# A two-layer attention and feed-forward kernel on one core: new planner order, spread weight loads, half-width exponentials in segment 0, and 30 matmuls on a constant tile at the start

## The chip, the cores and the metric

The kernel runs on one core of one Trainium2 chip. The metric is the device time of one execution in microseconds (us). The engines are named as the profile names them: PE (TensorE, matrix products; PEld is its weight load), ACT (ScalarE), DVE (VectorE), POOL (GpSimd) and SP (SyncE, which here issues loads, stores and transposing DMAs).

## The reference, cut to what matters

The input is 2048 tokens of width 512. Two layers are computed, with the same weights; each is an attention block followed by a gated feed-forward block, both with a layer norm in front and a residual behind:

```python
for layer in range(2):
    x = x + A(layernorm(x))      # 32 heads of width 16, 4 segments of 512 tokens
    x = x + B(layernorm(x))      # (silu(x w1) * (x w3)) w2, inner width 1376

def A(x):                         # per head
    q, k, v = x @ wq, x @ wk, x @ wv
    M, z = 0, 0                   # memory carried from segment to segment
    for s in range(4):
        p = softmax(q_s @ k_s.T / 4 + causal_mask)
        a_dot = p @ v_s
        a_mem = (phi(q_s) @ M) / (phi(q_s) @ z + 1e-6)    # phi(t) = t+1 if t>0 else exp(t)
        o_s = sigmoid(beta) * a_mem + (1 - sigmoid(beta)) * a_dot
        M, z = M + phi(k_s).T @ v_s, z + sum(phi(k_s))
    return concat(o_s) @ wo
```

## The kernel before, in words

Everything but the loads and the stores stays in SBUF. The work is cut into eight segments, numbered g = 0 to 7: four segments of 512 tokens in layer 0 and four in layer 1. A segment goes through these stages.

- **Layer norm** (`layer_norm`): DVE takes statistics of four tiles of 128 tokens (L502, L504, L507), POOL the inverse root (L509), DVE normalises (L515), and SP issues four transposing DMAs (L519) into `xa` (attention) or `xf` (feed-forward).
- **Projections** (`project`): 12 groups of four matmuls of 512 columns: four for `v` (L538), four for `q` and four for `k` (L543). ACT or DVE evicts each group (`ev`, L440 or L441). DVE makes two masked copies `km` of each `k` group (L558).
- **Memory** (`phi`, `memory_update`, `memory_read`): L564 to L645.
- **Attention** (`attention`): four head groups G, each of five *units*. One unit is a set of logits matmuls on PE (L674), one exponential of 128x2048 on ACT (L682), and one or two causal masks on POOL (L685). Two times in each G a *value group* of 16 matmuls on PE (L700) multiplies masked exponentials by `v`; the result `xs` is evicted, transposed by a DMA into `xg` (L710), divided by the row sum (L715, L718, L724), joined with the memory part (L733), and transposed by a DMA into `ot` (L735). Thus a segment has 20 units and 8 value groups.
- **Output projection** (`out_proj`, L743): 16 matmuls, then the residual on DVE (L746).
- **Feed-forward** (`ffn`): 88 matmuls for gate and up (L767), tanh on ACT (L775), two products on DVE (L777, L783), 44 matmuls down (L791), and the residual (L796). In layer 1 the result is stored by SP.

So a segment has 48 + 16 + 132 = 196 matmuls of 512 columns beside the attention units.

PSUM has two parts. Pool `S` is one slot of four banks, which holds the logits of one unit, so the next unit's logits can't be written before the exponential of the last one has been read. Pool `B` is four banks for everything else.

The order of each engine's instructions isn't written by hand. `Sched.schedule` is a list planner that runs when the kernel is built: each operation has a cost (`o_act`, `o_dve`, `o_pool`, `MM512`), a priority and possibly a *gate* (an operation that must have been placed before it), and the planner fixes one order for each engine. On the chip every engine goes through its order strictly, with semaphore waits where data is needed. An engine thus stops at a waiting instruction even if a later one could run. The planner interleaves the segments: PE fills the time of an exponential with matmuls of the projections of the next segment and of the feed-forward of earlier ones.

Loads before: the first four token tiles on SP's queue, `wq`, `wk`, `wv` and `betab` on ACT's queue at the same time (L431). `late_loads` issues everything else on POOL's queue as soon as the first transposed tiles are there: the other 12 token tiles, `wo`, `w1`, `w3`, `w2`, 6.3 MB in all. POOL then multiplies `w2` by 0.5 in place (L485, L487).

Of the kernel before, what the change touches and what calls it, by code (L numbers as in the profile page):

```python
# [13 lines left out]
H = 32  # L14
# [45 lines left out]
class Sched:  # L60
# [15 lines left out]
    def add(self, opts, fn, reads=(), writes=(), bufs=(), prio=0.0, mode=None, dmaq=None, name="", gates=(), size=0,  # L76
# [7 lines left out]
        op.issued = False  # L84
        op.eng = None
# [28 lines left out]
    def schedule(self):  # L114
# [23 lines left out]
        while left:  # L138
            best = None
            for e in ENGS:  # L140
# [3 lines left out]
                for op in avail[e]:  # L144
                    s = tf
# [180 lines left out]
def o_act(n, psum=True):  # L326
    return ("act", 114.0 + 0.833 * n, (190.0 if psum else 225.0) + 0.833 * n)


def o_dve(n, psum=False, mode=1.0):  # L330
    c = n / 0.96 / mode
    return ("dve", c + (75.0 if psum else 45.0), c + (150.0 if psum else 65.0))
# [13 lines left out]
def build(nc, A_x, A_wq, A_wk, A_wv, A_wo, A_beta, B_w1, B_w3, B_w2, out):  # L346
# [3 lines left out]
    def mkpool(name, n):  # L350
        pools[name] = Pool(name, n)
# [53 lines left out]
    mkpool("S", 1)  # L405
# [50 lines left out]
    for i in range(2):  # L456
        z = pool(lambda e, i=i: e.memset(va_r[i][:], 0.0), 3104, writes=[("va0", i)], prio=-50.0)
        o = pool(lambda e, i=i: e.memset(vheads(va_r[i], slice(0, LT), 0, H)[:, :, :, 16:17], 1.0), 128, writes=[("va0", i)], prio=-50.0)
        pools["va"].prev[i] = [z, o]

# [7 lines left out]
    ldw("act", wq_sb, A_wq, "wq", CP)  # L468
    ldw("act", wk_sb, A_wk, "wk", CP + 1)
    ldw("act", wv_sb, A_wv, "wv", CP + 2)  # L470
    dma("act", betab[:], A_beta.partition_broadcast(P), 8192, prio=CP + 3, writes=["betab"], name="ldbeta")

    def late_loads(after):
        for i in range(1, 4):
            dma("pool", x_tok[:, 4 * i:4 * i + 4, :], xv[:, 4 * i:4 * i + 4, :], 524288, prio=CP + i,
                reads=after, writes=[("x", 4 * i + j) for j in range(4)], name="ldx")
            if i == 1:
                ldw("pool", wo_sb, A_wo, "wo", CP + 1.5, reads=after)
        ldw("pool", w1_sb, B_w1, "w1", CP + 4, reads=after)
        ldw("pool", w3_sb, B_w3, "w3", CP + 5, reads=after)  # L480
        dma("pool", w2_sb[:, 0:10, :], B_w2[0:1280, :].rearrange("(t p) d -> p t d", p=P), 1310720, prio=CP + 6,
            reads=after, writes=["w2a"], name="ldw2")
        dma("pool", w2_sb[0:96, 10, :], B_w2[1280:1376, :], 98304, prio=CP + 7, reads=after, writes=["w2b"], name="ldw2")
        for a in range(2):
            pool(lambda e, a=a: e.tensor_scalar(w2_sb[:, 5 * a:5 * a + 5, :], w2_sb[:, 5 * a:5 * a + 5, :], 0.5, None, op0=ALU.mult),  # L485
                 2560, reads=["w2a"], writes=["w2a"], prio=0.9)
        pool(lambda e: e.tensor_scalar(w2_sb[0:96, 10, :], w2_sb[0:96, 10, :], 0.5, None, op0=ALU.mult), 512,  # L487
             reads=["w2b"], writes=["w2b"], prio=0.9)
# [7 lines left out]
    def layer_norm(s, name, prio, gates=(), fine=False):  # L496
# [3 lines left out]
        for i in range(LT):  # L500
            tt = 4 * s + i
            dve(lambda e, i=i, tt=tt: e.bn_stats(ln_r[st.slot][:, i, 0:6], x_tok[:, tt, :]), 512, reads=[("x", tt)],  # L502
# [9 lines left out]
        for i in range(LT):  # L512
            tt = 4 * s + i
            xn = new("xn")
            dve(lambda e, i=i, tt=tt, xn=xn: e.tensor_scalar(  # L515
                xn_r[xn.slot][:], x_tok[:, tt, :], ln_r[st.slot][:, i, 6:7], ln_r[st.slot][:, i, 9:10],
                op0=ALU.subtract, op1=ALU.mult), 512, mode=1.3, reads=[("x", tt), (st, 3, i), (st, 1, i)], writes=[(xn, 0)],
                bufs=[st, xn], prio=prio, name="norm")
# [8 lines left out]
    def project(s, g, X, first):  # L527
# [4 lines left out]
        for n, (kind, G) in enumerate(jobs):  # L532
            p0 = g - 0.95 + 0.05 * n
            B = new("B")
            for cg in range(NCG):
# [10 lines left out]
                pe(fn, MM512, reads=rd + ["w" + kind], writes=[(B, 0)], bufs=[B, X], prio=p0 + 0.001 * cg,  # L546
# [5 lines left out]
            else:  # L552
# [3 lines left out]
                if kind == "k":  # L556
                    for ee in range(2):
                        dve(lambda e, G=G, ee=ee: e.tensor_scalar(km_r[z.km.slot][:, ee, G, :], k_r[z.k.slot][:, G, :],  # L558
                                                                  cm[ee][:, 0:1], None, op0=ALU.mult), 512, mode=2.4,
# [3 lines left out]
    def phi(src, t, dst, dt_, prio):  # L563
        for hf in range(2):  # L564
# [6 lines left out]
                1024, mode=2.5, reads=rd, writes=[(dst, hf)], bufs=[src, dst], prio=prio, name="ph1")  # L571
# [3 lines left out]
                1024, mode=1.8, reads=[(x, 0), (dst, hf)], writes=[(dst, hf)], bufs=[x, dst], prio=prio, name="phmax")  # L575
# [286 lines left out]
```

The softmax here doesn't subtract the row's maximum and nothing guards it: scores larger than these inputs give would overflow.

## Time and profile before

| | |
|---|---|
| median of 3 runs | 563.25 us (562.81 to 563.76) |
| profiled execution | 562.49 us; span of the core's instructions 560.7 us |
| mean granted TensorE clock | 0.945 |
| busy share of the span | PE 86%, PEld 35%, DVE 79%, ACT 71%, POOL 42% |
| first exponential of each segment starts (us) | 20.5, 95.0, 153.3, 210.2, 263.2, 319.4, 373.2, 427.9 |
| last exponential starts | 479.9 us |

The first line is what comparisons are made against; the profiled execution is one execution of its own. A busy PE isn't a PE at its peak, since matmuls overlap and the granted clock can be half of the full one. The eight starts show how long each segment's attention lasts: 74.5 us for segment 0, 58.3 us for segment 1, and 52 to 57 us for the others. After the last exponential some 81 us remain, in which PE works off feed-forward blocks.

### The profile page before, as it was taken

The numbers are of one execution on the slowest core, as the hardware profiler recorded it, in microseconds if no ns is written. First come the engines' busy times: TensorE is split into PE (matmuls) and PEld (weight loads), VectorE is DVE, ScalarE is ACT, GpSimd is POOL, SyncE is SP. The second block draws the span as 40 slices with busy tenths as digits, with TensorE's granted clock in tenths as the row PEclk, the third lists the DMA queues.
The fourth block names the chain that finished last, engine by engine and source line by source line (L and its number), as shares of the span: only waits on it lengthen the run. The fifth ranks groups of instructions, "written<-read, shape, count | busy, mean of one in ns | idle before, by whom it ended". The sixth has DMA issues, their size and how long they took to land.

```text
span 560.7 us, 9831 instructions
## 1 busy us (share of the span) xinstructions
PE 484.8 (86%) x3836; PEld 198.4 (35%) x3904; DVE 445.5 (79%) x893; ACT 395.5 (71%) x324; POOL 235.2 (42%) x326
## 2 busy tenths in 40 slices
PE   1837568758999899999989999999999999989897
PEld 0212123222333333333333433443334433434343
DVE  4558999885769787898877989899987897868573
ACT  1736387877987799889878898888998798322130
POOL 7528843453435435545434544444454444210000
PEclk9956789877999899999999999999999999999999
DMA  5793112324211431143223231323113110220301
GB/s 169 243 275 75 39 39 47 49 49 94 39 29 30 67 67 29 29 85 58 47 39 67 49 67 39 67 48 67 39 39 85 48 40 19 67 66 1 76 0 39
DMA packets 106255, 35.31 MB, mean 63 GB/s; under 512 B 100736, under 2 KB 104832, under 8 KB 106208
## 3 DMA queue, kind: packets, MB, share of 16 engines
q1 hardware_dynamic: 102976, 26.76, 24.1%
q0 software_dynamic: 1504, 6.32, 3.2%
q10 hardware_dynamic: 1728, 1.58, 0.9%
q8 instruction: 31, 0.51, 0.4%
q14 instruction: 16, 0.13, 0.1%
HBM read 8.43 MB, written 2.10 MB: 19 GB/s over the span
## 4 chain that ended last, share of the span: by engine, by line
PE 48%; DVE 24%; DMA 11%; issue 7%; ACT 4%; POOL 4%; SPq 1%; POOLq 0%
PE psall L767 19%; PE psall L543 6%; PE psall L791 6%; DMA xg<-xs 5%; PE psall L674 5%; PE psall L700 5%; DVE xn L515 4%; ACT e L682 3%; PE psall L743 3%; PE psall L538 3%; DVE ln L502 2%; DMA ot<-og 2%; DMA pkt<-pk 1%; DVE x_tok L746 1%; DMA xf<-xn 1%
## 5 line engine op out<-in xcount | busy, mean ns | idle before, releaser
L682 ACT ACTIVATE e<-psall 128x2048 bf16<-128x2048 f32 x160 | 300.3, 1877 | 57.5 <-PE psall L674 55.1
L685 POOL TENSOR_SCALAR_AFFINE_SELECT e<-e 128x512 bf16<-128x512 bf16 x256 | 168.3, 675 | 205.7 <-ACT e L682 205.6
L767 PE MATMUL psall<-xf,w 128*128 128x512 bf16 (+1 forms) x678 | 172.5, 386 | 9.8 <-DMA xf<-xn 3.3
L767 PEld LDWEIGHTS psall<-xf,w 128*128 128x128 bf16 (+1 forms) x704 | 65.4, 101 | 90.1 <-issue 18.4
L775 ACT ACTIVATE th<-psall 128x512 bf16<-128x512 f32 (+1 forms) x88 | 52.0, 597 | 54.6 <-PE psall L767 54.5
L791 PE MATMUL psall<-w,h 128*128 128x512 bf16 (+1 forms) x334 | 87.2, 380 | 1.3 <-issue 0.8
L674 PE MATMUL psall<-q,km 32*128 32x512 bf16 (+3 forms) x1024 | 66.1, 313 | 16.0 <-ACT e L682 14.6
L777 DVE SCALAR_TENSOR_TENSOR gp<-th,psall 128x512 bf16<-128x512 bf16 (+1 forms) x88 | 59.1, 678 | 18.0 <-ACT th L775 17.4
L783 DVE TENSOR_TENSOR h<-gp,psall 128x512 bf16<-128x512 bf16 (+1 forms) x88 | 59.4, 678 | 9.2 <-PE psall L767 8.6
L700 PE MATMUL psall<-e,va 128*32 128x512 bf16 (+3 forms) x1024 | 49.2, 316 | 6.2 <-POOL e L685 5.4
L515 DVE TENSOR_SCALAR xn<-x_tok,ln 128x512 bf16<-128x512 bf16 x64 | 43.6, 713 | 12.2 <-POOL ln L509 7.6
L538 PE MATMUL psall<-wv,xa 128*128 128x512 bf16 x123 | 37.4, 418 | 14.6 <-DMA xa<-xn 13.7
L791 PEld LDWEIGHTS psall<-w,h 128*128 128x128 bf16 (+1 forms) x352 | 32.1, 98 | 38.1 <-issue 6.6
L674 PEld LDWEIGHTS psall<-q,km 32*128 32x128 bf16 x1024 | 18.0, 93 | 77.0 <-ACT e L682 66.0
L543 PE MATMUL psall<-xa,wk 128*128 128x512 bf16 x120 | 37.6, 404 | 6.8 <-DVE q L441 5.6
L502 DVE BATCH_NORM_STATS2 ln<-x_tok 128x6 f32<-128x512 bf16 x64 | 42.5, 675 | 0.4
L509 POOL TENSOR_TENSOR ln<-ln,mhalf 128x4 f32<-128x4 f32 (+1 forms) x19 | 18.2, 959 | 46.7 <-DVE ln L507 39.3
L700 PEld LDWEIGHTS psall<-e,va 128*32 128x32 bf16 x1024 | 22.3, 98 | 41.3 <-POOL e L685 21.6
L743 PE MATMUL psall<-wo,ot 128*128 128x512 bf16 x122 | 33.2, 398 | 3.6 <-DMA ot<-og 1.7
L543 PE MATMUL psall<-xa,wq 128*128 128x512 bf16 x123 | 34.2, 382 | 1.8 <-DVE va L441 1.1
L724 POOL TENSOR_TENSOR og<-xg,rd 128x256 bf16<-128x256 bf16 x27 | 20.4, 757 | 28.7 <-DVE rd L718 14.1
L796 DVE TENSOR_TENSOR x_tok<-psall,x_tok 128x512 bf16<-128x512 f32 x32 | 21.9, 684 | 13.2 <-PE psall L791 13.1
(61 smaller groups left out, 437.7 us busy)
## 6 DMA issues: line engine op xcount, KB each, us to landing
w<-in_B_w_dram POOLq DMA_DIRECT2D x2, 1376.0 KB, 11.0
out_dram<-x_tok SPq DMA_DIRECT2D x16, 128.0 KB, 1.8
x_tok<-in_A_x_dram POOLq DMA_DIRECT2D x3, 512.0 KB, 6.1
w<-in_B_w_dram POOLq DMA_DIRECT2D x1, 1280.0 KB, 16.3
xg<-xs SPq DMA_TRANSPOSE x64, 2.4
wq<-in_A_wq_dram ACTq DMA_DIRECT2D x1, 512.0 KB, 4.5
x_tok<-in_A_x_dram SPq DMA_DIRECT2D x4, 128.0 KB, 5.2
wk<-in_A_wk_dram ACTq DMA_DIRECT2D x1, 512.0 KB, 6.8
```

The costliest lines, as they stand in the source:

```text
L502: dve(lambda e, i=i, tt=tt: e.bn_stats(ln_r[st.slot][:, i, 0:6], x_tok[:, tt, :]), 512, reads=[("x", tt)], writes=[(st, 0, i)], bufs=[st], ...
L515: dve(lambda e, i=i, tt=tt, xn=xn: e.tensor_scalar(xn_r[xn.slot][:], x_tok[:, tt, :], ln_r[st.slot][:, i, 6:7], ln_r[st.slot][:, i, 9:10], ...
L538: fn = lambda e, cg=cg, G=G, B=B, st=st, sp_=sp_: e.matmul(bank(B), xa_r[X.slot][:, cg, 128 * G:128 * G + 128], wv_sb[:, cg, :], start=st, ...
L543: fn = lambda e, cg=cg, G=G, B=B, st=st, sp_=sp_, w=w: e.matmul(bank(B), w[:, cg, 128 * G:128 * G + 128], xa_r[X.slot][:, cg, :], start=st ...
L674: o = e.matmul(S4[:, pg, c:c + n], km_r[z.km.slot][32 * pg:32 * pg + 32, ee, G, 128 * j:128 * j + 128], q_r[z.q.slot][32 * pg:32 * pg + 32 ...
L682: act(lambda e, N=N, ebuf=ebuf: e.activation(e_r[ebuf.slot][:, :, 0:N], S4[:, :, 0:N], ACT.Exp, scale=SCALE), 4 * N, reads=[(sbuf_, 0)], w ...
L685: pool(lambda e, ebuf=ebuf, c=c: e.affine_select(e_r[ebuf.slot][:, :, c:c + 128], e_r[ebuf.slot][:, :, c:c + 128], pattern=[[0, 4], [1, 128]],
L700: o = e.matmul(bank(X)[32 * pg:32 * pg + 32, 128 * j:512], va_r[z.va.slot][:, j, VS * (8 * G + 2 * pg + ee):VS * (8 * G + 2 * pg + ee) + 3 ...
L767: prev = pe(lambda e, cg=cg, ft=ft, fw=fw, B=B, w=w: e.matmul(bank(B)[0:fw, :], w[:, cg, 128 * ft:128 * ft + fw], xf_r[X.slot][:, cg, :], ...
L777: dve(lambda e, fw=fw, B=B, th=th, gp=gp: e.scalar_tensor_tensor(gp_r[gp.slot][0:fw, :], th_r[th.slot][0:fw, :], 1.0, bank(B)[0:fw, :], AL ...
L783: dve(lambda e, fw=fw, B=B, gp=gp, h=hs[ft]: e.tensor_tensor(h_r[h.slot][0:fw, :], gp_r[gp.slot][0:fw, :], bank(B)[0:fw, :], ALU.mult), 51 ...
L791: prev = pe(lambda e, i=i, ft=ft, fw=fw, B=B, h=hs[ft]: e.matmul(bank(B), h_r[h.slot][0:fw, 128 * i:128 * i + 128], w2_sb[0:fw, ft, :], st ...
```

## The change

The main parts, in the order of the program:

- POOL clears only one of the two `va` buffers at the start, and DVE the other. DVE also sets one `h` buffer to 0.25, and 30 matmuls of 512 columns on that constant tile are PE's first instructions. Nothing reads their result.
- `wv`, `wq`, `wk` are issued on ACT's queue only when the four token tiles have landed, `betab` first. The load of `wo` moves to the head of POOL's queue.
- The other loads on POOL's queue are cut into smaller pieces and gated on units of segment 0, so that POOL issues them among its masks.
- The factor 0.5 moves from `w2` into the product that makes `h` (a `scalar_tensor_tensor` in place of a `tensor_tensor`); POOL's three multiplications fall away.
- Pool `S` gets two slots of two banks. In segment 0 each unit is cut in two halves: half of the logits matmuls, an exponential of 128x1024, then the other half. In all other segments a unit takes both slots, as before.
- Half of the joins with the memory part (L733) go to POOL by the planner's choice.
- The planner's costs, priorities and gates change, and so does the order on every engine, through all eight segments.

The core of the diff (the costs and priorities shown stand for some more of their kind):

```diff
-    mkpool("S", 1)
+    mkpool("S", 2)
...
-        z = pool(lambda e, i=i: e.memset(va_r[i][:], 0.0), 3104, writes=[("va0", i)], prio=-50.0)
+        z = (dve if i == 0 else pool)(lambda e, i=i: e.memset(va_r[i][:], 0.0), 3104, writes=[("va0", i)], prio=-50.0 if i == 0 else 0.5)
...
+    wset = dve(lambda e: e.memset(h_r[0][:], 0.25), 512, writes=["warm"], prio=CP - 1)
+    WS = new("S")
+    warm = [pe(lambda e: e.matmul(S4[:, 2 * WS.slot, :], h_r[0][:, 0:128], h_r[0][:], start=True, stop=True), 270.0,
+               reads=["warm"], bufs=[WS], prio=CP, name="warm") for _ in range(30)]
+    pools["h"].prev[0] = [wset] + warm
...
-    ldw("act", wq_sb, A_wq, "wq", CP)
-    ldw("act", wk_sb, A_wk, "wk", CP + 1)
-    ldw("act", wv_sb, A_wv, "wv", CP + 2)
+    x03 = [("x", i) for i in range(4)]
+    ldw("act", wv_sb, A_wv, "wv", CP, reads=x03)
+    ldw("act", wq_sb, A_wq, "wq", CP + 1, reads=x03)
+    ldw("act", wk_sb, A_wk, "wk", CP + 2, reads=x03)
...
+        for a in range(2):
+            dma("pool", w2_sb[:, 5 * a:5 * a + 5, :], B_w2[640 * a:640 * a + 640, :].rearrange("(t p) d -> p t d", p=P), 655360,
+                prio=CP + 6, gates=[units[(0, 13 + 2 * a)]], writes=["w2%d" % a], name="ldw2")
...
-            pool(lambda e, a=a: e.tensor_scalar(w2_sb[:, 5 * a:5 * a + 5, :], w2_sb[:, 5 * a:5 * a + 5, :], 0.5, None, op0=ALU.mult),
-                 2560, reads=["w2a"], writes=["w2a"], prio=0.9)
...
-                pe(fn, MM512, reads=rd + ["w" + kind], writes=[(B, 0)], bufs=[B, X], prio=p0 + 0.001 * cg,
+                pe(fn, MM512, reads=rd + ["w" + kind], writes=[(B, 0)], bufs=[B, X], prio=p0 + 0.001 * cg - 500, gates=[gate],
...
+                groups = [(0, 1), (2, 3)] if g in SPLIT else [(0, 1, 2, 3)]      # SPLIT = (0,)
+                for pgs in groups:
+                    sb_ = [new("S") for _ in range(len(pgs) // 2)]
...
+                    act(lambda e, N=N, ebuf=ebuf, pgs=pgs, sps=sps: e.activation(
+                        e_r[ebuf.slot][:, pgs[0]:pgs[-1] + 1, 0:N], S4[:, sps(pgs[0]):sps(pgs[-1]) + 1, 0:N], ACT.Exp, scale=SCALE),
+                        len(pgs) * N, reads=[(x, 0) for x in sb_], writes=[(ebuf, b[2], pgs[0]) for b in blocks],
+                        bufs=sb_ + [ebuf], prio=pr, name="exp")
...
-            pr = g + 0.25 * G
+            pr = g - 1 + 0.25 * G
...
-                dve(lambda e, fw=fw, B=B, gp=gp, h=hs[ft]: e.tensor_tensor(
-                    h_r[h.slot][0:fw, :], gp_r[gp.slot][0:fw, :], bank(B)[0:fw, :], ALU.mult), 512, True,
+                dve(lambda e, fw=fw, B=B, gp=gp, h=hs[ft]: e.scalar_tensor_tensor(
+                    h_r[h.slot][0:fw, :], gp_r[gp.slot][0:fw, :], 0.5, bank(B)[0:fw, :], ALU.mult, ALU.mult), 512, True,
...
-            X2 = layer_norm(s, "xf", g + 1.1)
+            X2 = layer_norm(s, "xf", g + 0.1)
```

## The prediction, made before the changed kernel ran

> **What bounds the kernel now.** I read first the span in 40 slices (the rows show tenths of busy time and of the granted clock).
>
> ```profile
> PE   1837568758999899999989999999999999989897
> ...
> ACT  1736387877987799889878898888998798322130
> ...
> PEclk9956789877999899999999999999999999999999
> ```
>
> From slice 11 (about 140 us) PE is busy nine tenths at full clock; before that it has holes and a low clock. So there are two regimes, and I looked at the early one by timeline and waits.
>
> ```profile
> 31.21 1.88 ACT L682 ACTIVATE e<-psall 128x2048 bf16<-128x2048 f32 x1 [0.72 <-PE psall L674]
> 40.94 1.88 ACT L682 ACTIVATE e<-psall 128x2048 bf16<-128x2048 f32 x1 [7.86 <-PE psall L674]
> ...
> 117.49 1.88 ACT L682 ACTIVATE e<-psall 128x2048 bf16<-128x2048 f32 x1 [0.50 <-PE psall L674]
> 119.87 1.88 ACT L682 ACTIVATE e<-psall 128x2048 bf16<-128x2048 f32 x1 [0.50 <-PE psall L674]
> ```
>
> The last pair shows the loop that one `S` slot makes: exponential, logits, exponential; 2.38 us at full clock, 0.50 of it idle. The first pair shows a hole of 7.86 us. Its cause is on PE and DVE:
>
> ```profile
> 39.26 1.09 PE L594 MATMUL psall<-va,pkt 128*128 128x136 bf16 x8 [8.10 <-DMA pkt<-pk]
> 65.88 1.89 PE L543 MATMUL psall<-xa,wk 128*128 128x512 bf16 x4 [5.57 <-DVE q L441]
> ```
> ```profile
> 58.48 6.74 DVE L515 TENSOR_SCALAR xn<-x_tok,ln 128x512 bf16<-128x512 bf16 x1
> 58.42 6.66 POOL L485 TENSOR_SCALAR w<-w 128x2560 bf16<-128x2560 bf16 x1
> ```
>
> A transposing DMA took 9.3 us while the late loads ran (issued from 17.2, last landing at 38.6), and two normalisations (0.40 us elsewhere) took nearly 7 us each beside POOL's two multiplications of `w2`. Segment 0 therefore lasts 74.5 us.
>
> The clock, by stretches of 5 us (after the span: PE, PEld, DVE, ACT, POOL busy, then the clock):
>
> ```profile
> 75.00:80.00 5.00, 2.06 (x36) 0.98 (x36) 5.00 (x11) 4.59 (x4) 2.34 (x3) 0.99 0.23 52
> 80.00:85.00 5.00, 3.53 (x30) 1.60 (x32) 3.78 (x8) 3.23 (x4) 1.94 (x3) 0.50 0.43 81
> ...
> 115.00:120.00 5.00, 2.42 (x40) 1.31 (x36) 5.00 (x17) 3.89 (x3) 2.74 (x4) 1.00 0.12 28
> 120.00:125.00 5.00, 2.42 (x31) 0.65 (x28) 4.85 (x12) 3.62 (x2) 3.08 (x5) 0.59 0.54 82
> ```
>
> Stretches with PE busy 41 to 54% are followed by half clock; over 70% kept it full.
>
> **A yardstick.** I cut the run into steps, from one unit's logits to the next. Prices at full clock: a unit 0.33 us on PE (142.54 to 142.87), a 512-column matmul 0.216 (the 16 of L743: 3.62 us, less a 0.38 tail, over 15), a value group 0.66 (148.59 to 149.25), memory matmuls 0.04 to 0.08. The loop is 1.82 us plus ACT's other work in that step (0.52 an eviction or tanh, 0.96 an L568), at least 2.38. A step costs the larger of PE's sum and the loop; I summed this over each segment, taking each engine's order from the built programs.
>
> | segment | before: 512-col matmuls, sum, measured | after: matmuls, sum |
> |---|---|---|
> | 0 | 93, 52.3, 74.5 | 69, 44.2 (halves, below) |
> | 1 | 110, 51.1, 58.3 | 92, 53.8 |
> | 2 | 170, 53.3, 56.9 | 152, 53.7 |
> | 3 | 164, 50.6, 53.0 | 170, 53.2 |
> | 4 | 174, 53.5, 56.2 | 154, 51.5 |
> | 5 | 173, 53.0, 53.8 | 158, 49.8 |
> | 6 | 169, 53.3, 54.7 | 228, 71.5 |
> | 7 | 164, 51.5, 52.0 | 142, 47.8 |
>
> (Segment 7 to its last unit.) So the sum is short by 22.2, 7.2, then 11.4 together for segments 2 to 7. After the last unit before has 325 matmuls, 72.8 us by the sum, 81.3 measured: 3.7 from the last matmul to the end, the rest DMA and DVE waits.
>
> **The change, part by part.**
>
> *Start.* The first `q` matmuls wait for the fourth transposed tile (16.92), the first logits follow 3.1 us later (20.05). Now the token tiles share the queues only with `wo`: the fourth landed at 9.08 among 2 MB of loads done at 9.61, so 1 MB should land near 5.5. The price of the new wait: `wv`, `wq`, `wk` go out about 5.5; 1.5 MB at that pace (2 MB in 8.8 us) is in by some 12.5, before `q` needs it; behind it on ACT stands only the first eviction. On DVE the statistics queue behind two memsets (between 0.5 and 3 us; POOL's took 2.69) and a reduction that waits for POOL, where `wo`'s issue (0.75) and a 2.68 memset stand ahead of the inverse roots. I get the roots from 7.2 to 9.7, the first normalised tile at 8.9, its transpose landing 2.5 later and the others 1.25 apart (as from 9.24 before), so the fourth at 15.2 and, 3.2 later, the first logits at **18.5** (17 to 20.5).
>
> *The 30 matmuls* start near 1.3 after the `h` memset. Clock went full 3.3 us after the first matmul (11.77 to 15.05), so about 8 run at 0.43 and 22 at 0.216: done by 9.6, before any `v` tile. They price at nothing, hidden by the load of x; if the clock stayed half they end at 14.2 and push `q` to 16.8, +1.6. They gain nothing either: `q` waits for the transpose, whatever the clock of the 12 `v` matmuls. The Trainium skill (TensorE: Matmul & The Clock Gate, "Why this matters for your kernels") advises 4 us of warm-up for measuring matmuls; by it the 12 would take 2.6 us instead of 5.2, which the same wait swallows.
>
> *Segment 0 in halves.* An exponential of 128x1024 isn't in the trace; ACT's 512 and 2048 forms (0.60, 1.88) give 1.02 by the line through them, L568 of that size starts its successor 0.95 later (22.27 to 23.22). With two slots the logits are ready during the other half, so a half costs the larger of 0.95 and PE's 0.33 plus fillers (mostly two matmuls, 0.76): 38.7 for 39 halves, two evictions 1.0, and the last step (16 `k` matmuls, a value group) 4.5: 44.2. The gating of loads and the missing `w2` products remove the 9.3, 6.7 and 6.7 us operations; each of ten load issues on POOL (0.75) is hidden by masks that have a step to spare, 7.5 if exposed. What is late next is the clock: PE's planned share is 75%, but twice (halves 11 to 14 and 33 to 38) it is 47%, and like the rows above I expect two spells of 6.8 us at half clock. There a half costs 0.55 + 2x0.43 = 1.41 against 0.95: 2.3 us a spell. With 0.4 for the second token load, **+5** (0 to 21.6: all at half clock, 65.8).
>
> The Trainium skill (same page, "Part 1: The HAM clock gate") says that the clock falls after an idle window of about 3.4 us. By that rule no spell would come, since no planned gap is over 0.7, and the sum would be 4.6 lower. The trace disagrees: after 115 to 120 the clock fell with no gap over 2.0.
>
> *Segment 1.* 53.8; before's excess of 7.2 came with 20 us at half clock, through units 4 to 12 with almost no matmuls between. After has such a lull only in units 6 to 8: **+4** (0 to 10).
>
> *Segments 2 to 7.* The DVE product that takes 0.5 costs nothing (L777 of the same form 678 ns, L783 678). Twelve joins move from DVE (517) to POOL (about 1.5, twice L724's 757), idle half of the time. Evictions on ACT are in the sums. Segment 6 holds one step with 94 matmuls and no unit, because segment 7's projections come late there. Sums 327.5; excess as before, **+11.4** (5 to 22).
>
> *After the last unit* 376 matmuls remain, 51 more: part of the gain is given back. 376x0.216 + 0.66 + 0.33 = 82.2, 3.7 for the end, 2 for the output projection, which has 13 us of other matmuls to cover a chain of about 13: **87.9** (86 to 92).
>
> Sum: 18.5 + 49.2 + 57.8 + 338.9 + 87.9 = 552.3, plus 1.8 around the span (562.49 - 560.7) = 554.1. The profiled run stands 0.8 below the median, so 555.
>
> **Rivals.**
>
> *Cold clock, slower.* If PE stays at half clock through segments 0 and 1, its 0.33, 0.216 and 0.66 become 0.55, 0.43 and 1.2. Segment 0 costs 65.8, +16.6; segment 1 has 37.9 us of PE work, twice of which is 75.8, +18. That is 589, slower; it decides from about 8 us lost, half of segment 0. For it: 75 and 70% planned, not far above 54. Against: at half clock PE is busy all the time, and after such a stretch (130 to 135, 4.41 of 5) the clock rose.
>
> *Gain given back, no change.* The end is a PE queue: if the order also loses 8 us at the new lull of segment 6 or in the tail, nothing is left: 563. For it: the tail grows by 9 us already. Against: PE's total work is the same and its early holes are real.
>
> *Better than that.* Costs nearer to the trace (`km` 428 ns measured, planned 267 before and 385 now, for 512 columns) could leave half of the 11.4 and no spells: 555 - 5.7 - 4.6 - 2 = 543.
>
> *Only the redesign works*: without effect of the 30 matmuls. That's my forecast, same time.
>
> **Numbers.** Forecast 0.70 (a few us around 555), better 0.08, no change 0.04, slower 0.18 (cold clock, whole or half). What a measurement of this kernel can tell is 0.2%, 1.1 us. Faster 0.78, same 0.04, slower 0.18. Range 541 to 568: the better case below, the first third of the cold clock above.
>
> **What would show it.** First exponential near 19; exponentials of 128x1024 near 1.02 us and 0.95 apart; segment 1 starting near 68; no DMA wait over 4 us and no DVE operation over 2 us before 70; the last exponential near 465 and some 88 us behind it. It is wrong if segment 0 lasts over 58 us or the segments after it take more than 57 each, segment 6 aside.

## The result, and the profile after

| | before | after |
|---|---|---|
| median, both kernels on the same chip | 563.03 us (560.27 to 563.76) | 585.01 us (582.02 to 589.52) |
| profiled execution, span | 562.49, 560.7 | 582.39, 580.7 |
| mean granted clock | 0.945 | 0.926 |

The change makes the kernel slower: ratio 1.0407, 95% interval 1.0317 to 1.0496. The forecast was 555.0, with a range of 541 to 568. (Ratios leave disturbed executions out, and the profile of one kernel below, the one with numerators back, loads at once and no 30 matmuls, is of such an execution: 543.76 us, where its three others took 535.59 to 536.11.)

Times by stage, each from the first exponential of one segment to that of the next; the last four columns are experiments that are explained below. The row on half clock counts what the profile records within the span; the records begin only at 15.05 us in before and at 6.07 in after.

| stage (us) | before | forecast | after | loads in a burst | numerators back, pieces kept | numerators after reciprocals | both causes undone, 30 kept |
|---|---|---|---|---|---|---|---|
| to the first logits | 20.1 | 18.5 | 23.3 | 23.3 | 23.6 | 21.7 | 19.9 |
| segment 0 | 74.5 | 49.2 | 61.3 | 51.4 | 65.0 | 62.1 | 42.7 |
| segment 1 | 58.3 | 57.8 | 60.3 | 60.3 | 58.0 | 58.9 | 63.0 |
| segments 2 to 7 | 326.6 | 338.9 | 348.4 | 348.1 | 322.5 | 325.6 | 325.1 |
| last exponential to the end | 80.9 | 87.9 | 86.9 | 86.8 | 83.6 | 85.9 | 84.6 |
| half clock, in all | 61.4 | | 86.5 | 62.2 | 62.3 | 45.6 | 24.7 |

Against before: 3.2 lost at the start, 13.2 won in segment 0, then 2.0, 21.8 and 6.0 lost: 19.8 of the span's 20.0. Against the forecast: +4.8, +12.1, +2.5, +9.5, -1.0.

The span of after in 40 slices of 14.5 us (tenths of busy time, and of the granted clock):

```profile
PE   6968976787999989999998998969999899999997
...
ACT  1674778688889778988998788967756878403130
...
PEclk9875678699899999999997999978999899999999
```

PE's early holes have become shallower, but the clock is low in slices 2 to 8, and there is a new low on ACT at slices 30 and 31 (5 and 6), where before had 9 and 8. The timeline shows both on ACT (start, duration, instruction, and in brackets the idle time before it with its releaser):

```profile
42.62 1.02 ACT L698 ACTIVATE e<-psall 128x1024 bf16<-128x1024 f32 x1 [0.48 <-PE psall L690]
47.77 1.02 ACT L698 ACTIVATE e<-psall 128x1024 bf16<-128x1024 f32 x1 [4.13 <-PE psall L690]
...
61.23 1.02 ACT L698 ACTIVATE e<-psall 128x1024 bf16<-128x1024 f32 x1 [0.48 <-PE psall L690]
62.73 1.02 ACT L698 ACTIVATE e<-psall 128x1024 bf16<-128x1024 f32 x1 [0.48 <-PE psall L690]
...
420.58 1.88 ACT L698 ACTIVATE e<-psall 128x2048 bf16<-128x2048 f32 x1 [0.62 <-PE psall L690]
442.94 1.88 ACT L698 ACTIVATE e<-psall 128x2048 bf16<-128x2048 f32 x1 [0.39 <-PE psall L690]
```

The halves take 1.02 us as forecast, and most start 0.90 after the one before where nothing holds them; but 61.23 and 62.73 are 1.5 apart. Between 422.46 and 442.94 no exponential runs at all: 20.5 us, the hole ahead of segment 7. In segment 0 the hole of 4.13 is one that PE passes on:

```profile
39.50 1.03 PE L547 MATMUL psall<-wv,xa 128*128 128x512 bf16 x2 [2.07 <-DMA xa<-xn]
...
46.16 1.03 PE L547 MATMUL psall<-wv,xa 128*128 128x512 bf16 x2 [3.58 <-DMA xa<-xn]
```

The projections of segment 1 wait for transposed tiles. And the clock, by 5 us (PE, PEld, DVE, ACT, POOL busy, the clock, DMA share, GB/s):

```profile
45.00:50.00 5.00, 3.84 (x17) 0.77 (x21) 1.20 (x4) 1.75 (x2) 0.00 (x0) 0.50 0.64 191
50.00:55.00 5.00, 5.00 (x30) 1.32 (x23) 2.46 (x5) 2.89 (x5) 2.72 (x4) 0.50 0.45 98
55.00:60.00 5.00, 5.00 (x33) 1.10 (x32) 3.12 (x11) 3.33 (x4) 1.23 (x2) 0.50 0.74 120
60.00:65.00 5.00, 5.00 (x16) 0.73 (x14) 3.17 (x8) 3.56 (x4) 3.97 (x5) 0.50 0.43 110
```

It is at half from 36.8 to 67.5, 30.7 us, although PE counts as busy without a break from 50 to 65. The start looks like this:

```profile
1.53 8.87 PE L464 MATMUL psall<-h 128*128 128x512 bf16 x30 [1.53 <-DVE mhalf L447]
15.12 5.02 PE L547 MATMUL psall<-wv,xa 128*128 128x512 bf16 x12 [4.71 <-DMA xa<-xn]
```

The 30 matmuls end at 10.4, PE then idles for 4.71, the clock falls at 12.9, and the 12 `v` matmuls take 5.02 us, half clock. The warmth is lost before it is used.

### The profile page after: what moved, and what is told of

It reads as the page before. It is cut to its first block, busy times and chain, and to the rows that moved or that the text cites. A ratio compares the mean times of both kernels' runs of the same rounds, so it can differ in the third digit from the quotient of the medians.

```text
span 580.7 us, 9976 instructions
## 1 busy us (share of the span) xinstructions
PE 521.7 (90%) x3934; PEld 204.8 (35%) x3934; DVE 432.5 (74%) x875; ACT 400.0 (69%) x350; POOL 236.3 (41%) x339
## 4 chain that ended last, share of the span: by engine, by line
PE 56%; DVE 21%; DMA 10%; ACT 8%; POOL 3%; issue 2%; SPq 0%; DVEq 0%
PE psall L785 18%; PE psall L809 11%; PE psall L552 6%; ACT e L698 6%; PE psall L690 6%; PE psall L718 5%; PE psall L761 4%; PE psall L547 4%; DMA xg<-xs 4%; DMA xa<-xn 3%; DMA ot<-og 2%; DVE km L567 2%; DVE h L801 2%; DVE ln L510 2%; DVE q L442 1%
## 5 line engine op out<-in xcount | busy, mean ns | idle before, releaser
L698 ACT ACTIVATE e<-psall 128x2048 bf16<-128x2048 f32 (+1 forms) x180 | 301.4, 1696 | 65.2 <-PE psall L690 61.8
L785 PE MATMUL psall<-xf,w 128*128 128x512 bf16 (+1 forms) x704 | 174.9, 387 | 2.4 <-DVE gp L795 1.4
L690 PE MATMUL psall<-q,km 32*128 32x512 bf16 (+3 forms) x1024 | 76.6, 318 | 16.3 <-ACT e L698 14.7
L809 PE MATMUL psall<-w,h 128*128 128x512 bf16 (+1 forms) x352 | 83.9, 380 | 0.7 <-DVE rm L631 0.7
L801 DVE SCALAR_TENSOR_TENSOR h<-gp,psall 128x512 bf16<-128x512 bf16 (+1 forms) x88 | 59.4, 678 | 9.3 <-PE psall L785 9.0
L718 PE MATMUL psall<-e,va 128*32 128x512 bf16 (+3 forms) x1024 | 51.6, 328 | 10.4 <-POOL e L703 3.6
L690 PEld LDWEIGHTS psall<-q,km 32*128 32x128 bf16 x1024 | 20.1, 93 | 88.5 <-ACT e L698 65.2
L547 PE MATMUL psall<-wv,xa 128*128 128x512 bf16 x128 | 39.9, 431 | 11.9 <-DMA xa<-xn 11.9
L510 DVE BATCH_NORM_STATS2 ln<-x_tok 128x6 f32<-128x512 bf16 x64 | 42.7, 679 | 1.9 <-DMA x_tok<-in_A_x_dram 1.4
L552 PE MATMUL psall<-xa,wq 128*128 128x512 bf16 x128 | 37.9, 405 | 0.1
L567 DVE TENSOR_SCALAR km<-k,cm 128x512 bf16<-128x512 bf16 x64 | 26.4, 440 | 14.8 <-ACT k L441 14.8
L523 DVE TENSOR_SCALAR xn<-x_tok,ln 128x512 bf16<-128x512 bf16 x64 | 30.1, 500 | 2.1 <-POOL ln L517 1.8
```

The source lines that it names most:

```text
L547: fn = lambda e, cg=cg, G=G, B=B, st=st, sp_=sp_: e.matmul(bank(B), xa_r[X.slot][:, cg, 128 * G:128 * G + 128], wv_sb[:, cg, :], start=st, ...
L552: fn = lambda e, cg=cg, G=G, B=B, st=st, sp_=sp_, w=w: e.matmul(bank(B), w[:, cg, 128 * G:128 * G + 128], xa_r[X.slot][:, cg, :], start=st ...
L690: o = e.matmul(S4[:, sps(pg), c:c + n], km_r[z.km.slot][32 * pg:32 * pg + 32, ee, G, 128 * j:128 * j + 128], q_r[z.q.slot][32 * pg:32 * pg ...
L698: act(lambda e, N=N, ebuf=ebuf, pgs=pgs, sps=sps: e.activation(e_r[ebuf.slot][:, pgs[0]:pgs[-1] + 1, 0:N], S4[:, sps(pgs[0]):sps(pgs[-1]) ...
L718: o = e.matmul(bank(X)[32 * pg:32 * pg + 32, 128 * j:512], va_r[z.va.slot][:, j, VS * (8 * G + 2 * pg + ee):VS * (8 * G + 2 * pg + ee) + 3 ...
L785: prev = pe(lambda e, cg=cg, ft=ft, fw=fw, B=B, w=w: e.matmul(bank(B)[0:fw, :], w[:, cg, 128 * ft:128 * ft + fw], xf_r[X.slot][:, cg, :], ...
```

## The experiments

**Theory first held:** segment 0 lost its gain because waiting loads now run beside the transposing DMAs, and the holes hold the clock down. **Rivals:** the 30 matmuls cost by running; the planner's order alone is the cause.

### The 30 matmuls made thin

```diff
-    S4[:, 2 * WS.slot, :], h_r[0][:, 0:128], h_r[0][:]
+    S4[:, 2 * WS.slot, 0:1], h_r[0][:, 0:128], h_r[0][:, 0:1]
```

> The changed kernel with the 30 constant matmuls cut from 512 columns to one, and the same order on every engine. Theory 'the warm-up is spent before it is needed' (in the changed kernel the clock is full from 6.1 to 12.9 us and half again from 12.9 to 19.7, while the first v matmul starts at 15.1): the time stays within 0.5% of the changed kernel (582 to 588), first logits at 23.3 +- 0.7. Rival 'the 30 matmuls shift the clock for the worse in segment 0': the long half-clock spell (36.8 to 67.5) is shorter and the time falls by 5 us or more.

586.79 us (580.14 to 589.24), ratio to before 1.0399 (1.0334 to 1.0464), with the same order on every engine: within the expected time, so what the 30 do by running neither helps nor hurts the total. Two things came otherwise. The first logits were at 22.1, earlier than the expected 23.3 +- 0.7. And the long spell at half clock was shorter, 17.1 us in place of 30.7; within segment 0 the clock was at half for 26.3 us in place of 37.5, yet the segment took 62.3 us (61.3 in after). So, in these two profiles, the time at half clock alone doesn't set segment 0.

### The weights issued first again

```diff
-    ldw("act", wv_sb, A_wv, "wv", CP, reads=x03)
+    ldw("act", wv_sb, A_wv, "wv", CP)
```
(and so for `wq`, `wk`; the load of `wo` goes behind units)

> The changed kernel with wv, wq and wk issued at once at the start (no wait for the token tiles) and wo's load gated into segment 0; PE's order is unchanged. Theory 'the waiting weight loads collide with the first four transposing DMAs' (6.2 us each instead of 2.5): transposes take 2.5 us again, the first logits come at 18.5 to 20.5 instead of 23.3, and the time falls by 3 to 5 us. Rival 'something later sets the end and takes it back': the first logits come earlier but the time stays within 1 us of the changed kernel.

581.84 us (579.11 to 588.93), ratio 1.0334 (1.0287 to 1.0381). The first four transposes went from 6.2, 5.3, 4.4, 3.5 us to 2.5 each and the first projection from 15.1 to 10.5, but the first logits only from 23.3 to 22.7, not the expected 18.5 to 20.5. The 3.2 us less in the median are more than that and lie within the spread of both kernels. A new wait took the place of the old one; DVE's timeline of this run shows it:

```profile
9.20 0.69 DVE L510 BATCH_NORM_STATS2 ln<-x_tok 128x6 f32<-128x512 bf16 x1
12.28 0.18 DVE L498 TENSOR_SCALAR gg<-gth 128x32 f32<-128x32 f32 x1 [2.40 <-ACT gth L497]
```

The 8 KB of `betab` now came behind the weights, and the tanh of it on ACT behind an eviction; DVE waited, and the third and fourth tile behind it were transposed only from 14.3 on. So the start was a collision and hides another wait.

### All late loads at once

```diff
-                reads=after if i == 1 else (), gates=[] if i == 1 else [units[(0, 8 * i - 9)]],
+                reads=after,
```
(and so for `wo`, `w1`, `w3`, `w2`; the planner then makes another order)

> The changed kernel with all late loads issued in one burst as soon as the first transposed tiles are there, as before the change, in the changed kernel's pieces; the planner's order differs in places. Theory 'the pieces spread over segment 0 collide with the transposes that feed segment 1's v projections, PE stands, and the clock falls': with the burst over near 40 us, transposes after that take 2.5 us, the holes of 3.6 and 5.2 us among the exponentials at 37 to 48 us shrink below 2 us in total, and segment 0 (first exponential to segment 1's first) falls from 61 to 48 to 54 us. Rival 'the clock falls because half-width units leave PE idle': segment 0 stays at 58 to 63 with half clock for 20 us or more.

556.90 us (554.68 to 566.02), ratio 0.9921 (0.9883 to 0.9959): 0.8% faster than before. Segment 0 takes 42.4 us in place of 61.3, less than the expected 48 to 54, with half clock of 44.4 in all. ACT's timeline shows a stretch of it as the forecast had thought all of it:

```profile
45.82 9.45 ACT L698 ACTIVATE e<-psall 128x1024 bf16<-128x1024 f32 x10
```

But the order had changed as well: the hole ahead of segment 7 was 14.6 in place of 20.5.

### The redesign without the 30 matmuls

```diff
-    wset = dve(lambda e: e.memset(h_r[0][:], 0.25), 512, writes=["warm"], prio=CP - 1)
-    WS = new("S")
-    warm = [pe(...
-    pools["h"].prev[0] = [wset] + warm
```

> The changed kernel without the 30 matmuls and their memset. The planner's order changes too: the longest stretch of matmuls without a unit before segment 7 shrinks from 98 to 45 matmuls, 401 instead of 376 remain after the last unit. Theory 'the order lets attention run ahead of the feed-forward, so that segment 7 waits for layer 0's last block': the stretch without an exponential before segment 7 falls from 20 to about 10 us, the tail grows by 25 matmuls (5.4 us), and the time is 576 to 584. Theory 'the 30 matmuls themselves cost the time': 570 or less.

565.97 us (564.71 to 575.07), ratio 1.0065 (1.0039 to 1.0092): 19.0 less than after, and still no faster than before. The time lies in the range that was given to "the 30 matmuls themselves cost the time", but running them costs nothing (the thin ones showed that), so these 19 us come through the planner, by more than the first theory had (576 to 584): it counts 270 ns for each, every later choice is made at another planned time, and the longest run of matmuls without an exponential is 45 without them and 98 with them. By stage, segment 6 takes 12.4 us less and segment 0 7.0 less; the tail takes 3.5 more.

### The loads in a burst, the order kept

```diff
         self.schedule()
+        for seq in (self.order["pool"], self.issue):
+            late = [op for op in seq if op.dmaq == "pool" and op.name != "ldwo"]
+            at = seq.index(late[0])
+            for op in late:
+                seq.remove(op)
+            seq[at:at] = late
         self.finalize()
```

> The changed kernel with every instruction of TensorE, VectorE and ScalarE in the order that it has there, the 30 constant matmuls too. Only the late loads move: on GpSimd's queue the pieces of x, w1, w3 and w2 are emitted together, right behind the first of them, in place of one by one along segment 0. Theory 'collisions' (segment 0's holes and its cold clock come from load pieces that run beside the DMA transposes of that segment): no later transpose over 5 us, segment 0 falls from 61 us to 43 to 50, the half clock from 88 us in all to 45 to 65, and the time to 565 to 572. Theory 'order alone' (the sequence of matmuls sets segment 0 too): segment 0 stays at 58 to 62 and the time at 579 to 585. By both, the hole of about 20 us ahead of segment 7 stays, because the order does.

574.42 us (572.02 to 578.80), ratio 1.0251 (1.0181 to 1.0321). This tells load timing from order. The time lies between the two theories. Segment 0 went from 61.3 to 51.4, a little short of the expected 50; every other stage stayed within 1 us, the hole of 20.5 too. How the tile `xa` fares between 30 and 55 us, first in after, then here (waits for it in us and times; DMA from issue to landing):

```profile
  DMA xa<-xn: 12.3, 4
...
DMA to landing us min/median/max: 4.5/7.6/8.4
```
```profile
  DMA xa<-xn: 1.3, 2
...
DMA to landing us min/median/max: 2.4/2.5/2.8
```

The same four transposes, issued from 34.9 and 34.8 us on, take a third as long when no load is issued beside them (in after one of 512 KB at 37.48, landing at 41.66, and two of 688 KB at 38.25 and 40.13, landing at 46.15 and 48.44). The clock still falls at the same place (37.1, after 36.8), so the holes don't start the cold spell. It lasts 13.7 us in place of 30.7; that the collisions lengthen it isn't shown, since it lasted 17.1 with the thin matmuls, whose order and loads are those of after. Collisions are worth 10.6 us; they aren't the larger part of the loss.

### The factor of 0.5 alone, in the kernel before

```diff
-    h_r[h.slot][0:fw, :], gp_r[gp.slot][0:fw, :], bank(B)[0:fw, :], ALU.mult), 512, True,
+    h_r[h.slot][0:fw, :], gp_r[gp.slot][0:fw, :], 0.5, bank(B)[0:fw, :], ALU.mult, ALU.mult), 512, True,
...
-            pool(lambda e, a=a: e.tensor_scalar(w2_sb[:, 5 * a:5 * a + 5, :], ..., 0.5, None, op0=ALU.mult),
```

> The kernel before with one part of the change alone: the factor 0.5 of the gate goes into the feed-forward product on VectorE, and GpSimd's multiplications of w2 are left out. Theory 'shared path' (VectorE's two long operations of about 6.7 us, in the time of GpSimd's multiplications, are what holds segments 0 and 1 of before): no VectorE operation over 3 us ahead of 100 us, segment 0 falls from 74.5 us by 8 to 13, time 549 to 555. Rival 'covered' (the late xa transposes or the next loads end the same waits): the two long operations go, but segments 0 and 1 together keep their 132.8 us within 3, time 560 to 565. Slower by over 1% would mean that the product with its constant costs more than the plain one, at about 0.05 us for each of 88.

551.95 us (550.53 to 552.91), ratio 0.9823 (0.9776 to 0.9870). Segment 0 takes 66.5 in place of 74.5, as expected, and the normalisation that took 6.74 us takes 0.40:

```profile
55.20 0.40 DVE L510 TENSOR_SCALAR xn<-x_tok,ln 128x512 bf16<-128x512 bf16 x1
```

This smallest part of the change, alone, is worth 10 us (the planner makes another order on every engine here too, and its share isn't separated). So the parts are not bad; something else in the whole takes more than they give.

### The numerators' priority back, loads at once, no 30 matmuls

```diff
-    ... hold=[om], prio=g + 0.12 + 0.1 * G - 800, name="mnum")
+    ... hold=[om], prio=g + 0.12 + 0.1 * G, name="mnum")
```

> The kernel with loads at once (556.9 us), less two things: the 30 constant matmuls and their memset go, and the numerator matmuls lose the priority of -800 that the change gave them, so that they are queued again by their segment's time. Counted in the order, the tail after the last exponential is 368 matmuls and no stretch between two exponential units has more than 13, in place of one of 98. Theory 'order' (what remains lost in segments 2 to 7 is that ScalarE stands idle while a long run of matmuls is at TensorE): the hole of 14.6 us ahead of segment 7 falls under 5, segment 6 from 71.9 us to 52 to 57, and by the sum of the larger of both engines' work for each unit (11.4 us less) the time is 543 to 549. Rival 'TensorE's total' (the matmuls are as many, so what is not in the hole is spread over the others): segments 2 to 7 keep their sum of 342 within 4 and the time stays at 554 to 559.

535.92 us (535.59 to 543.76), ratio 0.9538 (0.9487 to 0.9588): the fastest kernel of this study, 7 us below the expected range. The hole is gone (no gap over 3.3 us), segment 6 takes 54.5 for 71.9. In the profile segment 0 takes 49.5 us, with a spell of 23.9 us at half clock.

### Loads at once, no halves, no 30 matmuls

```diff
-    SPLIT = (0,)
+    SPLIT = ()
```

> The kernel with loads at once, without the 30 constant matmuls and without the halves: segment 0's 20 units go whole through one S tile of four banks as in all other segments. Theory 'halves pay': ScalarE and TensorE take turns on the one tile, segment 0 comes to 49 to 54 us against 42.4, and with the order's sums of the other segments (506.5 against 504.3 in all) the time is 558 to 564. Rival 'halves are idle' (segment 0 is bound by its projections and its loads): segment 0 stays at 41 to 45 and the time at 553 to 558.

565.82 us (563.15 to 568.75), ratio 1.0075 (1.0041 to 1.0109). Segment 0 takes 58.7, more than the expected 49 to 54, against 42.4 in "all late loads at once", which has the halves. That fits halves that pay, but what part of the 16 us is theirs isn't separated: the 42.4 is of a kernel with the 30 matmuls and of another order, and segment 0 has 21.5 us of half clock here, 6.8 there. What the profile shows for the loop with one slot is that a unit isn't under 2.38 us:

```profile
52.33 1.88 ACT L693 ACTIVATE e<-psall 128x2048 bf16<-128x2048 f32 x1 [0.50 <-PE psall L685]
```

### The numerators' priority back, alone

The same one-line edit as above in the changed kernel; its 30 matmuls and its loads in pieces stay.

> The changed kernel with one number undone: the numerator matmuls are queued by their segment's time again, without the -800. The 30 constant matmuls and the loads piece by piece stay. Counted in the order, the longest run of matmuls between two exponential units goes from 98 to 16, layer 0's last feed-forward of segment 3 ends 68 units after that segment's start in place of 80, and the sum of the larger of both engines' work is 490.4 us against 507.6. Theory 'order': the hole of 20.5 us ahead of segment 7 falls under 5, segment 6 from 78.9 us to 52 to 58, segment 0 stays at 58 to 63, and the time is 562 to 569. Rival 'the order only moves the loss' (TensorE's matmuls are as many, and the collisions of segment 0 are the rest): time 575 to 585.

556.42 us (548.68 to 559.35), where the kernel before ran in 561.93 (559.25 to 563.33). One number in one line is worth 28.6 us by the medians, more than the 17 counted in the order, and below the expected 562 to 569: segment 6 falls from 78.9 to 55.3, and from segment 2 on no gap between exponentials is over 2.3. The low of ACT at slices 30 and 31 is gone:

```profile
ACT  1584677888878898987899778988889888222130
```

Segment 0 is no better (65.0; four transposes of `xa` took up to 11.3 us, and the clock stood at half for 47.8 us). So the order is the larger cause, and undoing it pays with the collisions still there.

### The numerators kept early, but after the reciprocals

Why do four matmuls per group matter? A numerator writes a bank of pool `B` and keeps it until the product L649, which needs the reciprocal of the denominators. The two kinds had nearly the same priority, but a numerator needs only half of the keys' memory and the denominators both halves. PE's and DVE's timelines of after:

```profile
170.40 0.41 PE L645 MATMUL psall<-mb,pq 128*128 128x128 bf16 x4
182.84 0.41 PE L645 MATMUL psall<-mb,pq 128*128 128x128 bf16 x4
191.02 0.59 PE L626 MATMUL psall<-mb,pq 128*128 128x8 bf16 x16
```
```profile
194.65 0.31 DVE L634 TENSOR_TENSOR rm<-rm,gg 128x128 f32<-128x128 f32 x1
194.99 1.89 DVE L649 TENSOR_TENSOR om<-psall,rm 128x512 bf16<-128x512 f32 x3
```

The first numerator runs 20.6 us ahead of the denominators (L626) and its bank is free 25.3 us after it was written, at 195.7 (the first third of 1.89); the second holds another for 13.5. Two of four banks are out of use. Added up over the 24 numerators (start of L645 to end of L649, in order), banks are held for 250.3 us in after, 73.6 before, 63.7 with the priority back. The edit keeps the early priority and lets the planner place a numerator only after its reciprocals:

```diff
-        dve(lambda e: e.tensor_tensor(rm_r[rm.slot][:, 2, :, :], ...
+        ready = dve(lambda e: e.tensor_tensor(rm_r[rm.slot][:, 2, :, :], ...
...
-    ... prio=g + 0.12 + 0.1 * G - 800, name="mnum")
+    ... prio=g + 0.12 + 0.1 * G - 800, gates=[ready], name="mnum")
```

> The changed kernel with its priority of -800 kept for the numerator matmuls, but each of them planned only after the reciprocals that its product on VectorE needs. In the changed kernel's trace a numerator holds its PSUM bank from its matmuls to that product, 250 us summed over 24 numerators and up to 25 us for one, since numerators run 15 and 20 us ahead of the denominators; with the priority undone the sum was 63 us. Theory 'held banks' (banks that wait for the reciprocals are what keeps the feed-forward back until 98 matmuls stand ahead of segment 7): the sum of holds falls under 80 us, the hole of 20.5 us under 5, segment 6 from 78.9 us to 52 to 58, and the time to 552 to 563, about that of the kernel with the priority undone (556.4). Rival 'the early place itself' (numerators ahead of projections and feed-forward delay them, whatever the banks): a hole over 8 us stays, time 570 to 585.

555.41 us (550.10 to 558.75), ratio 0.9851 (0.9813 to 0.9888). The holds sum to 54.6 us, no gap after segment 0 is over 2.7, segment 6 takes 54.7. Here the numerator follows its denominators:

```profile
189.10 0.58 PE L626 MATMUL psall<-mb,pq 128*128 128x8 bf16 x16
192.53 0.41 PE L645 MATMUL psall<-mb,pq 128*128 128x128 bf16 x4
```
```profile
195.63 1.87 DVE L649 TENSOR_TENSOR om<-psall,rm 128x512 bf16<-128x512 f32 x3
```

So it isn't the priority as such: with it kept, and numerators placed only when their bank is soon read, the loss is gone. The gate also moves them later (192.5 for 170.4), so a numerator that is early without holding a bank was not run. Nor do the holds alone set the size of the hole: they sum to 252.7 us with all late loads at once, where it is 14.6, and to 258.5 without the 30 matmuls, where it is 9.6. But the two go together through all kernels here: where the holds sum to 54 to 74 us, no gap ahead of segment 7 is over 3 us, and where they sum to 249 to 266, it is 9.6 to 20.5. The orders show how a hold becomes the hole: in after, segment 0's gate and up matmuls are spread over units 32 to 55, with free banks 32 to 44; layer 0's last feed-forward ends 80 units after its segment began, 68 with the priority back. Segment 7 needs that result exactly 80 units after segment 3, and finds 98 matmuls ahead of its first unit. A gap of 12.6 us at 71.6 in segment 0 remains. It belongs to the loads: DVE stands for 10.5 us there until a transposing DMA lands that was issued beside three of them.

```profile
77.01 0.35 DVE L733 RECIPROCAL rd<-xg 128x32 f32<-128x32 bf16 x1 [10.52 <-DMA xg<-xs]
```

### The 30 matmuls in a good order

"Numerators back, loads at once", with the 30 matmuls put back; all of PE's other instructions come in the same order.

> The kernel with loads at once and the numerator's priority undone (535.9 us), with the 30 constant matmuls put back. All of TensorE's other instructions come in the same order, so what the 30 do by running is seen alone. Theory 'they matter only through the order': within 3 us of 535.9, 533 to 539. Rival 'the clock that they raise pays': no half clock beside the first projections, segment 0 under 41 us, time 528 to 532. Rival 'they draw the clock down or delay the first projections': first logits after 22 us, time 541 to 548.

541.12 us (536.93 to 548.13), ratio 0.9608 (0.9530 to 0.9687), against 535.92 (0.9538, 0.9487 to 0.9588) without them. The intervals overlap: no gain is seen, and a loss of some us can't be excluded. The 541.12 lies outside the expected 533 to 539 and in the range of the second rival, whose sign, first logits after 22 us, didn't come (19.9). It is the kernel after with both causes undone, 43.9 us faster than after; the single steps add up to 10.6 + 28.6 = 39.2, and the start is 3.4 earlier here. With the numerators back and the loads at once, the planner also gives PE's other instructions one and the same order with and without the 30, so the 19.0 us that they cost in after hang on the rest of the plan. Its slices:

```profile
PE   7969877788999989989999999999989999999997
...
ACT  1799989688887979869898799988989797122130
...
PEclk9888979799999999999999999999999999999999
```

ACT is busy from slice 2 on, and the low ahead of segment 7 is gone.

### Start and order mended

"Numerators back, loads at once" with the weights issued at once and `betab` ahead of them.

> The kernel of 535.9 us with its start undone too: the three weight loads go out at once, as in the kernel before, and the load of beta goes ahead of them, because its 8 KB were late and held up the first layer norm when only the weights were moved. TensorE's order is the same. Theory: the first four transposes take 2.5 us each, the first projection comes by 11 us in place of 12.6, the first logits by 18.0 to 19.2 in place of 20.2, the time 532.5 to 535. Rival 'another wait takes its place' (the first four transposes are issued later, by the layer norm): first logits at 20 to 22, time 535 to 538.

538.39 us (535.84 to 544.50), ratio 0.9570 (0.9526 to 0.9613). The first logits came at 18.8, as expected, 1.4 earlier; the total shows no gain over 535.92, the intervals overlap. The expected 532.5 to 535 was missed, and 1.4 us is less than the executions of these kernels spread.

## Why the prediction was wrong

**What bounds the kernel.** The two regimes were read rightly, and the pieces named as gains are gains: the product with 0.5 (10 us alone), and probably the halves (segment 0 takes 42.4 us with them and 58.7 without, in kernels that differ in their order too). One row was read a little wrongly: of the two long normalisations the first took 6.29, the second 6.74. What was wrong is what the whole does with them.

**Start, 18.5 against 23.3.** The first transpose was issued at 8.85, as worked out (8.9). The failed step is "its transpose landing 2.5 later": the first took 6.2, because `wv`, `wq`, `wk`, held back until the tokens were there, went out at 6.9 to 7.9 and ran beside it (the tokens landed at 6.92, beside `wo`, not near 5.5). The price of that wait was looked for on ACT's queue and at `q`, not at the transposes. With the weights first the transposes took 2.5 again, but another wait, for `betab`, held the logits at 22.7; with that mended too, and the loads at once, they came at 18.8.

**The 30 matmuls, "They price at nothing".** Their running does (thin ones and "in a good order"), and their warmth is swallowed, if not quite by the wait that was named: the clock fell in a gap of 4.71. But they are 30 operations with a planned cost, and in this plan, by way of its order, they cost 19.0 us. The term was counted in the yardstick's order and never set apart there.

**Segment 0, 44.2 + 5 against 61.3: the largest miss.** The 5 is the mis-sized term: 17.1 came. "The gating of loads and the missing `w2` products remove the 9.3, 6.7 and 6.7 us operations" is the step that failed, in its first part. The gating brought new ones: in the first 110 us 15 transposes took over 4 us, where before had 6, since POOL issued its pieces next to those of segment 1's tiles. That is worth 9.9 us in segment 0: in the same order with the loads in a burst it took 51.4, which is 2.2 over the forecast. (The 44.2 itself was not measured in this order; 42.4 and 42.7 are of other orders with the loads at once.) The two forecast spells of 6.8 us at half clock were one of 30.7 and one of 6.8; in the burst they were 13.7 and 6.8. What the longer spell adds isn't shown, since the thin matmuls had 11 us less of half clock in this segment and no gain.

**Segment 1** was 60.3 for 57.8, within its bounds.

**Segments 2 to 7, 338.9 against 348.4.** The sum of 327.5 saw the hole (segment 6, 71.5) but took it as given; the failed step is "excess as before": 20.9 came in place of 11.4, of which 7.3 in segment 5 and 7.4 in segment 6. Spells at half clock stand there (6.8 us from 306.4, 10.2 from 384.9), but what part is theirs isn't separated. Against a sum of 315.2 for before, 12.3 us of loss were on the table in the forecast's own yardstick, and 9.4 more in the tail; they were set against a gain of 25.3 in segment 0, of which 13.2 came. With the priority of one kind of matmul back, segments 2 to 7 took 322.5. Asking why one step holds 94 matmuls (98 in the order) could have led there.

**The tail, 87.9 against 86.9**, was right.

**The rivals.** The cold clock was right in direction for segment 0 (65.8 if all of it were cold) and wrong in segment 1, where +18 was priced and 2.5 measured. The reason given against it fell: "at half clock PE is busy all the time, and after such a stretch (130 to 135, 4.41 of 5) the clock rose"; here it stayed down through 15 us of busy PE, and in before PE was busy for only 0.61 us of 30 to 35, at half clock. The Trainium skill (TensorE: Matmul & The Clock Gate, "Part 1: The HAM clock gate") lets the clock rise after one busy window of about 3.4 us; the rows of 50 to 65 don't agree, if PE was as busy as the profile counts it, which includes modelled ends. "Gain given back" named the right place, segment 6 and the tail, at too low a price. "Only the redesign works" isn't so either: without the 30 matmuls the kernel took 565.97 us, 19.0 less than with them and no faster than before.

**Still open:** why the clock, once down, stays so long in one profile (30.7, and 47.8 with the priority back) and not in another (17.1 with the thin matmuls); and how much of segment 0's remaining spread between kernels of the same order is that.

## What to carry to other kernels

When a planner fixes the order, any added operation with a cost can change every later choice, so compare the orders for long runs of one engine's work and ask which held buffer made them. Work done early is only free if what it occupies is soon given back: look from each producer to the moment its bank is read, and gate it on the last of its consumer's inputs. Spread loads out only where no latency-bound DMA stands beside them; here a burst that was nearly over before the next transposes was better than pieces (51.4 us against 61.3 in segment 0).

## What the runs showed of the hardware

- A transposing DMA that takes 2.5 us alone took 7.6 in the median and up to 8.4 while a plain load of 512 KB and two of 688 KB were under way, issued on another engine's queue (up to 12.9 in another run, "the weights issued first again", beside loads of these sizes).
- The granted clock fell at 36.8 us without a gap of PE over 0.53 us in the 8 us ahead of it; PE had been busy 1.82 of the last 3.40 us. It then stayed at half for 30.7 us, of which PE counts as busy for 15 without a break.
- A VectorE normalisation of 128x512 took 6.74 us in the time of a POOL product of 128x2560 (6.66 us), and 0.40 where those products are left out.
